# Reciprocal deviations in two halves of three rows, in a kernel with a written-out order for every engine

## The chip, the cores and the metric

The kernel runs on one core of a Trainium2 chip. A core has a matrix engine (TensorE, PE in the profile, with its weight loads as PEld), three engines for element-wise work (VectorE, DVE; ScalarE, ACT; GpSimd, POOL), a sync engine (SP) that here issues every transfer, and 16 DMA engines. The engines run their own instruction streams and meet at semaphores. The metric is the device time of one execution in microseconds (us); lower is better.

## The reference: chunk-selected attention, then a gated MLP

The inputs are q, k and v of 4 batches, 8 heads, 768 positions and 64 elements per head, and the weights of a gated MLP. The reference computes, cut to what matters:

```python
k_min, k_max = k_chunks.min(3), k_chunks.max(3)          # chunks of 32 positions
ub = maximum(q * k_min, q * k_max).sum(-1)                # bound per query and chunk
sel = the 6 chunks with the highest ub, causal            # per query
attn = softmax(where(sel & causal, q @ k.T / 8, -1e9)) @ v
x = attn with its 8 heads side by side                    # 4 x 768 x 512
u, v = halves of gelu_tanh(x @ w_in)                      # 512 columns each
v_n = (v - mean(v)) / sqrt(var(v) + 1e-6) * g_ln          # per row of 512
out = x + (u * (w_sg @ v_n + b_sg)) @ w_out
```

The change concerns `1 / sqrt(var(v) + 1e-6)`: one number for each of the 768 rows of a batch. On the chip these are 6 columns of 128 partitions, a tile of 128x6.

## The kernel before

**Pairs.** The 32 (batch, head) combinations are worked off as 16 pairs of heads, 4 pairs to a batch. For a pair the kernel loads q, k and v, transposes k and q on PE (`kside`, `qside`; both through `rows_T`, line 545), copies the transposed tiles out of PSUM on ACT or DVE (`evac`, lines 451 and 454), takes minimum and maximum per chunk on DVE (line 643, four reductions for a pair), subtracts them on POOL (`wsub`, line 662), takes max(q, 0) on POOL (`rel`, line 676) and casts q to bf16 on POOL (`qcast`, line 683). `select` and `select_full` then do the bound `ub` on PE (line 713 for pairs 0 to 3, line 760 for the later ones, which go two at a time), transpose it (lines 723 and 769), find the sixth-highest value (lines 730 and 780), compare (736, 785) and transpose back into the mask `Dt` (740, 788). The scores follow on PE (lines 874 and 880, or 834), exp on ACT (889 or 840), the zeroing above the diagonal on POOL (896, 845), the product with v on PE (912, 919), and the division by the sum on DVE (927, 929).

**Batches.** After its four pairs, a batch goes through `moe_h` and `moe_g`: the v half of the first matmul on PE (line 961, six row tiles), gelu on ACT (965), the statistics on DVE (970 and 972), variance plus epsilon on DVE (974), the power of -0.5 on POOL (976), and on DVE the normalised rows `vhat` (996), one instruction for each of the six row tiles. The u half is line 1007 on PE and 1012 on ACT. Then comes the spatial matmul on PE (1024), which reads all six `vhat` tiles, its scaling and gating on DVE (1042, 1046), the output matmul on PE (1058), the residual addition on DVE (1067) and the store (1072). The output of the last row tile of the last batch is written in two halves of 256 columns.

**Stores of PSUM.** The scores have two PSUM tiles of their own (PSC); everything else on PE shares four (PSG). Which step takes which is a written-out list (`slots`).

**The order.** Nothing is ordered by the loops alone. Each step is a numbered op, made by `P.op` with its engine, what it reads and what it writes. `TABLE` holds for each of the five queues (pe, act, dve, pool, sp) the list of op numbers in the order in which that engine runs them, and `P.link` puts a semaphore wait wherever an op needs another engine's result. An engine therefore never passes a step that waits. Before the first k transpose PE runs ten spare matmuls on a zeroed tile (`filler`, line 376).

**The start.** POOL makes constant tiles: among them a mask tile `INDF` (line 418), a bf16 identity `identB` (line 387) and some zeroed rows (line 810). In the list of POOL these stand between the steps of pairs 0 and 1: op 91 (cast of q, pair 1), 90 (`rel`, pair 1), 209 (zeroing, line 810), 8 (`identB`), 16 (`INDF`), 85 (`wsub`, pair 1), 108 (`wsub`, pair 2). In PE's list op 184, the third of the six scores steps of pair 0, stands just ahead of op 93, the bound of pair 1.

**Numbers of the ops.** `moe_h` makes two ops for the deviations of a batch in the kernel before (`var` and `rstd`), so that each op behind them in the program has the same number in every queue's list.

Of the kernel before, what the change touches and what calls it, by code (L numbers as in the profile page):

```python
# [6 lines left out]
ALU = mybir.AluOpType  # L7
# [253 lines left out]
def _build(nc, ctx, q, k, v, w_in, g_ln, w_sg, b_sg, w_out, out):  # L261
# [60 lines left out]
    INIT2 = 0  # L322
    K2R = "dma"
# [153 lines left out]
    def wsg_load(j):  # L477
# [4 lines left out]
        if WSGT == "f32":  # L482
            for hf in range(2):
                t = ps_g.tile((0, 1, 2, 3))

                def tr(e, t=t, dst=dst, hf=hf):
                    for x in range(3):
# [7 lines left out]
                     [("wsgT", j, hf)], [t], 1)  # L495
            return
# [455 lines left out]
    def moe_h(b):  # L952
# [3 lines left out]
        for qt in range(NT):  # L956
            t = ps_g.tile((0, 1, 2, 3))

            def hv(e, t=t, qt=qt):
# [14 lines left out]
        P.op("dve", lambda d: d.tensor_scalar(rstd[s][:], mv[s][:, :, 1], 1e-6, None, op0=ALU.add), (75, 150),  # L974
             ("var", b), reads=[("mv", s, qt) for qt in range(NT)], writes=[("rstd", s)])
        P.op("pool", lambda g: g.tensor_tensor(rstd[s][:], rstd[s][:], neghalf[:], op=ALU.pow), (1290, 1340),
             ("rstd", b), reads=[("rstd", s), "neghalf"], writes=[("rstd", s)])
# [6 lines left out]
        for qt in range(NT):  # L984
# [10 lines left out]
            else:  # L995
# [3 lines left out]
                     (456, 548), ("vhat", b, qt), port=True, reads=[("vg", qt), ("mv", s, qt), ("rstd", s)],  # L999
# [16 lines left out]
    def moe_g(b):  # L1016
        s = b % 2
        for tg in range(2):
# [31 lines left out]
            for qt in range(3 * tg, 3 * tg + 3):  # L1050
                cuts = (0, DM // 2, DM) if LAST and (b, qt) == (B - 1, NT - 1) else (0, DM)
                for x, (c0, c1) in enumerate(zip(cuts, cuts[1:])):
# [19 lines left out]
                    P.op("sp", lambda e, qt=qt, ob=ob, c0=c0, c1=c1: e.dma_start(  # L1072
# [48 lines left out]
    for p in range(4, NP + 4):  # L1121
# [38 lines left out]
    "act": (  # L1160
# [10 lines left out]
    "dve": (  # L1171
# [99 lines left out]
```

## Time and profile before

| what | value |
|---|---|
| runs | 213.49 us median of 3 (213.32 to 213.72) |
| the profiled execution's own time | 213.23 us |
| its span, first to last instruction | 211.5 us |
| around the span | 1.7 us |
| granted TensorE clock, mean over the span | 1.000 |
| PE, DVE, ACT, POOL busy | 94%, 87%, 71%, 50% of the span |

The page gives the busy time of each engine and the costliest groups of instructions, by line of the kernel. The view of windows gives busy time for stretches of the span. The view of waits says which line waited for which other engine's line, in total, how often, and the longest. The chain is followed back from the last instruction. The timeline lists start and length of merged runs of instructions, with the idle time ahead of them in square brackets. In rows of groups, "x24" is a count, and a row such as "128x6 f32<-128x6 f32" gives output and input shapes. A busy PE in the profile includes the time in which its matmuls are pipelined.

### The profile page before, as it was taken

Reading aid. Unit: us, or ns where it says so; the run is one execution under the profiler, and the core shown is the slowest. Engines: PE = TensorE matmul, PEld = TensorE weight load, DVE = VectorE, ACT = ScalarE, POOL = GpSimd, SP = SyncE. Lnnn points to the kernel's source line nnn. Section 1 sums busy time; section 2 is a strip of 40 time slices with the busy share of each in tenths; the row PEclk is TensorE's granted clock in tenths of the full one; section 3 lists DMA queues with packets and bytes.
Section 4 is the critical chain, followed back from the end, with each engine's and each line's share of the span. In section 5 each row is a group of like instructions: output and inputs, shape, how many; then the busy total and the mean of one; then the engine's idle time right before and its main releaser. Section 6 shows DMA issues by size and latency. Waiting matters only on the chain.

```text
span 211.5 us, 5892 instructions
## 1 busy us (share of the span) xinstructions
PE 198.9 (94%) x2319; PEld 133.8 (63%) x2319; DVE 184.1 (87%) x523; ACT 150.1 (71%) x227; POOL 105.4 (50%) x157
## 2 busy tenths in 40 slices
PE   7778989889999999999999999999997999999993
PEld 2455757755676668788456777787454777545652
DVE  4597998879999999899999999997599488788994
ACT  2786989947797668799849698999858886263000
POOL 5563967799615849675631754294583143001000
PEclk9999999999999999999999999999999999999999
DMA  7999999999059997949899899648633512410136
GB/s 147 218 218 197 286 198 288 330 276 230 1 150 253 230 239 203 221 104 267 199 180 221 175 227 226 153 122 113 128 86 62 129 37 40 152 47 10 42 149 248
DMA packets 94266, 35.96 MB, mean 170 GB/s; under 512 B 87584, under 2 KB 89376, under 8 KB 94240
## 3 DMA queue, kind: packets, MB, share of 16 engines
q1 hardware_dynamic: 94240, 35.60, 75.8%
q8 instruction: 18, 0.29, 0.6%
q14 instruction: 8, 0.07, 0.1%
HBM read 24.82 MB, written 6.34 MB: 147 GB/s over the span
## 4 chain that ended last, share of the span: by engine, by line
PE 76%; ACT 11%; POOL 5%; DMA 2%; DVE 2%; issue 1%; SPq 1%; DVEq 0%
PE PSG L1024 15%; PE PSC L834 12%; PE PSG L1007 10%; PE PSG L1058 9%; PE PSG L961 8%; PE PSG L545 7%; ACT E L889 5%; PE PSG L912 5%; PE PSG L760 3%; PE PSG L919 2%; ACT KA L451 2%; PE PSC L874 1%; ACT IND L415 1%; PE PSG L713 1%; DMA Wg<-scr_dram 1%
## 5 line engine op out<-in xcount | busy, mean ns | idle before, releaser
L840 ACT ACTIVATE E<-PSC 128x1024 bf16<-128x1024 f32 (+1 forms) x72 | 63.0, 924 | 9.7 <-PE PSC L834 9.4
L834 PE MATMUL PSC<-QA,KA 128*128 128x128 bf16 (+2 forms) x336 | 38.2, 246 | 1.6 <-ACT E L840 1.5
L1024 PE MATMUL PSG<-wsgT,vhat 128*128 128x384 bf16 x192 | 34.3, 326 | 0.0
L643 DVE TENSOR_REDUCE W<-PSG 128x12 f32<-128x384 f32 x56 | 28.0, 543 | 4.3 <-PE PSG L545 4.3
L834 PEld LDWEIGHTS PSC<-QA,KA 128*128 128x128 bf16 x336 | 24.1, 98 | 9.8 <-ACT E L840 4.3
L845 POOL TENSOR_SCALAR_AFFINE_SELECT E<-E 128x768 bf16<-128x768 bf16 x24 | 20.5, 864 | 19.6 <-ACT E L840 19.4
L683 POOL CAST QA<-qT 64x768 bf16<-64x768 f32 (+1 forms) x28 | 24.1, 864 | 9.4 <-PE PSC L834 4.9
L1012 ACT ACTIVATE uT<-PSG 128x384 bf16<-128x384 f32 x32 | 15.1, 489 | 17.5 <-PE PSG L1007 17.4
L1024 PEld LDWEIGHTS PSG<-wsgT,vhat 128*128 128x128 bf16 x192 | 18.4, 98 | 10.7
L1058 PE MATMUL PSG<-woutb,uT 128*128 128x512 bf16 (+1 forms) x100 | 23.8, 371 | 0.0
L889 ACT ACTIVATE E<-PSC 128x1024 bf16<-128x1024 f32 (+1 forms) x24 | 21.0, 916 | 3.6 <-PE PSC L880 3.4
L1007 PE MATMUL PSG<-xT,winb 128*128 128x384 bf16 x128 | 23.4, 326 | 0.0
L961 PE MATMUL PSG<-winb,xT 128*128 128x512 bf16 x96 | 22.5, 380 | 1.0 <-DVE U L775 0.7
L965 ACT ACTIVATE vgb<-PSG 128x512 f32<-128x512 f32 x24 | 14.1, 598 | 12.1 <-PE PSG L961 12.1
L1042 DVE SCALAR_TENSOR_TENSOR PSG<-PSG,glnT,bsgbc 128x384 f32<-128x384 f32 x32 | 19.5, 617 | 2.8 <-PE PSG L1024 2.6
L912 PE MATMUL PSG<-vx,E 128*128 128x65 bf16 x480 | 19.7, 194 | 0.0
L912 PEld LDWEIGHTS PSG<-vx,E 128*128 128x128 bf16 x480 | 17.8, 97 | 1.8 <-DVE XS L929 0.2
L970 DVE BATCH_NORM_STATS2 stats<-vgb 128x6 f32<-128x512 f32 x24 | 15.9, 682 | 3.1 <-ACT vgb L965 2.8
L929 DVE TENSOR_TENSOR XS<-PSG,rden 128x384 bf16<-128x384 f32 x32 | 17.5, 551 | 0.7
L1007 PEld LDWEIGHTS PSG<-xT,winb 128*128 128x128 bf16 x128 | 12.2, 98 | 9.0 <-ACT uT L1012 0.9
L451 ACT ACTIVATE KA<-PSG 128x384 bf16<-128x384 f32 (+1 forms) x34 | 16.5, 492 | 1.7 <-DVE W L643 1.6
L1046 DVE TENSOR_TENSOR uT<-PSG,uT 128x384 bf16<-128x384 f32 x32 | 16.9, 551 | 0.5
(93 smaller groups left out, 342.4 us busy)
## 6 DMA issues: line engine op xcount, KB each, us to landing
kn<-in_k_dram SPq DMA_DIRECT2D x32, 192.0 KB, 4.4
qn<-in_q_dram SPq DMA_DIRECT2D x32, 192.0 KB, 4.5
vn<-in_v_dram SPq DMA_DIRECT2D x16, 384.0 KB, 5.4
out_dram<-osb SPq DMA_DIRECT2D x18, 256.0 KB, 2.6
uT<-in_moe_w_sg_dram SPq DMA_DIRECT2D x4, 384.0 KB, 5.0
vgb<-in_moe_w_in_dram SPq DMA_DIRECT2D x3, 512.0 KB, 7.6
out_dram<-vgb SPq DMA_DIRECT2D x5, 256.0 KB, 2.1
QA<-Dt SPq DMA_DIRECT2D x24, 36.0 KB, 2.2
```

The lines of the kernel that those rows point to most:

```text
L451: P.op("act", lambda e: e.activation(dst(), src(), ACTF.Copy), act(n), tag, reads=reads, writes=writes, ps=ps, shift=shift)
L643: P.op("dve", lambda d, m=m, op=op, src=src, h0=h0, h1=h1: d.tensor_reduce(W[w][:, m, 12 * h0:12 * h1].rearrange("p (h c) -> p h c", h=h1 ...
L683: P.op("pool", lambda g, i=i, r0=r0, r1=r1: g.tensor_copy(QA[w][i or 0][r0:r1, :], qT[r][r0:r1, :]), gps(S, 250 if i == 1 else 150), ("qca ...
L834: r = e.matmul(t.ap()[:, o:o + n], KA[w][i][:, 128 * kb:128 * kb + 128], QA[w][i][:, q0:q0 + n], start=True, stop=True)
L840: P.op("act", lambda e, t=t, c0=c0, c1=c1, i=i: e.activation(E[es][:, i, c0:c1], t.ap()[:, 0:c1 - c0], ACTF.Exp, scale=SCALE), act(c1 - c0 ...
L845: P.op("pool", lambda g, ev=ev: g.affine_select(ev, ev, pattern=[[0, NT], [1, 128]], compare_op=ALU.is_ge, fill=0.0, base=0, channel_multi ...
L889: P.op("act", lambda e, t=t, c0=c0, c1=c1, n=n: e.activation(E[es][:, :, c0:c1], t.ap().rearrange("p (i x) -> p i x", i=2)[:, :, 0:n], ACT ...
L912: r = e.matmul(t.ap()[:, 65 * qb:65 * qb + 65], E[es][:, i, a:a + 128], vx[w][:, kb, i, :], start=first, stop=False, skip_group_check=True)
L961: r = e.matmul(t.ap()[:, 0:F], xT[s][:, dk, 128 * qt:128 * qt + 128], winb[:, dk, F:DFF], start=(dk == 0), stop=(dk == NDK - 1))
L1007: r = e.matmul(t.ap()[:, 0:TG], winb[:, dk, 128 * fb:128 * fb + 128], xT[s][:, dk, TG * tg:TG * tg + TG], start=(dk == 0), stop=(dk == NDK ...
L1024: r = e.matmul(t.ap()[:, 0:TG], vhat[s][:, sb, 128 * fb:128 * fb + 128], wsgT[:, sb, TG * tg:TG * tg + TG], start=(sb == 0), stop=(sb == N ...
L1058: r = e.matmul(t.ap()[:, 0:c1 - c0], gT[s][:, fb, 128 * qt:128 * qt + 128], woutb[:, fb, c0:c1], start=(fb == 0), stop=(fb == NF - 1))
```

## The change

The variance op and the power op of a batch are each replaced by two ops, for row tiles 0 to 2 and 3 to 5, and each `vhat` instruction now depends on its own half only. There are therefore four ops per batch instead of two, 8 more in all (1308 instead of 1300), and the numbers of all ops behind the first batch's deviations shift by 2, behind the second's by 4, and so on. Two further lists that are added (`WSTD`, `STQ`) are empty, so the code that they guard makes no op. The lists of all five queues, the PSUM slots and the filler (11 spare matmuls instead of 10) are new.

```diff
+    LNG = ((0, 3), (3, 6))
+    WSTD = ()
+    STQ = ()
...
-        P.op("dve", lambda d: d.tensor_scalar(rstd[s][:], mv[s][:, :, 1], 1e-6, None, op0=ALU.add), (75, 150),
-             ("var", b), reads=[("mv", s, qt) for qt in range(NT)], writes=[("rstd", s)])
-        P.op("pool", lambda g: g.tensor_tensor(rstd[s][:], rstd[s][:], neghalf[:], op=ALU.pow), (1290, 1340),
-             ("rstd", b), reads=[("rstd", s), "neghalf"], writes=[("rstd", s)])
+        for a0, a1 in LNG:
+            rn = [("rstd", s, qt) for qt in range(a0, a1)]
+            P.op("dve", lambda d, a0=a0, a1=a1: d.tensor_scalar(rstd[s][:, a0:a1], mv[s][:, a0:a1, 1], 1e-6, None, op0=ALU.add),
+                 (75, 150), ("var", b, a0), reads=[("mv", s, qt) for qt in range(a0, a1)], writes=rn)
+            P.op("pool", lambda g, a0=a0, a1=a1: g.tensor_tensor(rstd[s][:, a0:a1], rstd[s][:, a0:a1], neghalf[:, a0:a1], op=ALU.pow),
+                 (200 + 190 * (a1 - a0), 250 + 190 * (a1 - a0)), ("rstd", b, a0), reads=rn + ["neghalf"], writes=rn)
...
-                     (456, 548), ("vhat", b, qt), port=True, reads=[("vg", qt), ("mv", s, qt), ("rstd", s)],
+                     (456, 548), ("vhat", b, qt), port=True, reads=[("vg", qt), ("mv", s, qt), ("rstd", s, qt)],
...
     "pool": (
-        "5 11 4 6 2 20 3 326 21 12 19 56 51 57 7 91 90 209 8 16 85 108 197 113 58 196 114 164 159 128 249 165 "
...
+        "2 11 3 12 20 4 19 21 6 56 51 5 57 90 85 7 16 197 108 91 113 114 58 165 164 196 261 159 207 92 248 "
...
-        "47:10 77:2"),
+        "47:11 77:2"),
```

In the lists, the steps that the prediction speaks of stand as follows. (The names are those of the ops' tags: `kmm` a reduction of line 643, `hv` and `hu` the matmuls of lines 961 and 1007, `wst` the transpose of a tile of w_sg.)

| queue | before | after |
|---|---|---|
| POOL, pair 1 | cast of q, `rel`, zeroing, `identB`, `INDF`, `wsub` | `rel`, `wsub`, zeroing, `INDF`, a diagonal of pair 0, `wsub` of pair 2, cast of q |
| DVE, pairs 0 and 1 | compare of pair 0, its back transpose, two `kmm` of pair 1 (with one of pair 2 between) | compare of pair 0, `kmm` of pair 1, back transpose of pair 0, `kmm` of pair 1 |
| PE, pair 1 | scores step 184 of pair 0, then the bound of pair 1 | the bound of pair 1, then that scores step |
| SP, start | k, k, q, q of pair 0 | k, q, k, q of pair 0 |
| PE, batch 0 | `hu`, then the sixth `hv` | two `hu` and a `wst`, then the sixth `hv`, then that `hu` |
| POOL, batch 0 | w_sg cast 4, power, w_sg cast 5 | w_sg cast 4, a cast of q, power of the first half, w_sg cast 5, power of the second half |
| POOL, select of pairs 14, 15 | copies `wmin`, `wsub`, then `rel` of pair 15, `wmin`, `wsub` | `rel` of pair 15 and four other steps first, then the four copies together |
| SP, select of pairs 14, 15 | four loads of `Wg` follow the third x transpose | a load of v stands ahead of them |
| DVE, batch 3 | six statistics, variance, an addition (line 1067), six `vhat`, two additions | variance of the first half after four statistics, two `vhat` among the rest, variance of the second half, an addition, the last three `vhat`, two additions |
| PE and DVE, end | row tile 4, then the second half of row tile 5 | the second half of row tile 5, then row tile 4 |

More of the change, by code (lines that the diff above doesn't have):

```diff
@@ L495, in wsg_load @@
                      [("wsgT", j, hf)], [t], 1)
+            return
+        if j in WSTD:
+            wb = vhat[0][:].rearrange("p a b -> p (a b)")[:, S * (j % 4):S * (j % 4) + S]
+            wn = [("vhat", 0, y) for y in range(S * (j % 4) // F, (S * (j % 4) + S - 1) // F + 1)] + [("wv", j % 4)]
+            cast(wb, dst, S, ("wsc", j), [("stg", j % 4)] + names, wn)
+            P.op("sp", lambda e: e.dma_start(wsgT[:, :, 128 * j:128 * j + 128], wb, transpose=True), dmac(TRI), ("wtr", j),
+                 reads=wn, writes=[("wsgT", j, hf) for hf in range(2)], dma=f"trw{j}", xfer=TRX)
             return
@@ L1071, in moe_g @@
                         reads=[t] + [("XS", b % 2, hh) for hh in range(c0 // 64, c1 // 64)] + ([("vg", qt)] if x else []), writes=on, ps=[t])
-                    P.op("sp", lambda e, qt=qt, ob=ob, c0=c0, c1=c1: e.dma_start(
+                    P.op("act" if b in STQ else "sp", lambda e, qt=qt, ob=ob, c0=c0, c1=c1: e.dma_start(
                         bass.AP(out.tensor, (b * S + 128 * qt) * DM + c0, [[DM, 128], [1, c1 - c0]]), ob[:, c0:c1]), dmac(),
@@ L1143 @@
     "pe": (
[16 rows of a table removed]
-    "act": (
[10 rows of a table removed]
-    "dve": (
[17 rows of a table removed]
-    "pool": (
[14 rows of a table removed]
[16 rows of a table added]
+    "act": (
[10 rows of a table added]
+    "dve": (
[17 rows of a table added]
+    "pool": (
[15 rows of a table added]
     "slots": (
-        "1032323020021303233221230011010031120221010100231021031011000330001010010233121033010211230223301210"
-        "3203312003101011201131111010101232023111010033313011001101302220120223131002232210323032110230110100"
-        "3020000001113132310210011131131010010301021021113331320232031210300311101100021100111111000031100110"
-        "23203231130003222312023012101231"),
+        "3210103201021020001323021211010123310021110000321022031011002330203010010133130021011210023233121310"
+        "2201332112001011200120001110010332132111010033312311001101302322020222032113011330013032130012010100"
+        "3120010111013032320210011013121010011322021023131313002103233210312032101100231100110211100010101100"
+        "12220210110220312100320312131203"),
     "filler": (
-        "47:10 77:2"),
+        "47:11 77:2"),
 }
```

111 rows, old and new, of the table TABLE are left out of this document.

## The prediction

> **What bounds the kernel now.** I began with busy time by stretch of the span, from the view of windows. The columns are the length, then the busy time of PE, PEld, DVE, ACT and POOL, the granted clock, the DMA share and the GB/s.
>
> ```profile
> 5.00:47.00 42.00, 36.11 (x634) 26.06 (x632) 35.69 (x112) 34.37 (x52) 29.39 (x45) 1.00 1.14 254
> 47.00:145.00 98.00, 97.97 (x1147) 69.79 (x1146) 94.21 (x279) 79.66 (x124) 55.89 (x77) 1.00 0.90 187
> 145.00:165.00 20.00, 17.84 (x172) 10.28 (x171) 14.99 (x51) 16.10 (x25) 11.73 (x19) 1.00 0.43 93
> 165.00:208.30 43.30, 43.28 (x363) 26.29 (x360) 36.47 (x74) 18.73 (x27) 6.07 (x7) 1.00 0.28 85
> ```
>
> PE is the bound from 47 to 145 and from 165 to 208.3: 97.97 of 98.00 and 43.28 of 43.30. There an edit can only lose. Its idle time lies in the first 47 us (42.00 - 36.11 = 5.9 between 5 and 47) and between 145 and 165 (2.2). Next came the view of waits for PE, first from 5 to 50, then from 145 to the end (total, times, longest).
>
> ```profile
> PE PSG L713 <- POOL W L662: 1.8, 2, 1.2
> PE PSC L874 <- ACT E L889: 1.3, 2, 0.7
> ```
>
> ```profile
> PE PSC L834 <- ACT E L840: 1.5, 1, 1.5
> PE PSG L760 <- POOL W L618: 0.3, 1, 0.3
> ```
>
> None of these names the deviations. What waits for them is in the view of the tile `rstd` (min/median/max in ns, then the first and last start):
>
> ```profile
> L974 DVE TENSOR_SCALAR rstd<-mv x4: 170/174/406, 56.0 to 189.6; 128x6 f32<-128x6 f32 x4
> L976 POOL TENSOR_TENSOR rstd<-rstd,neghalf x4: 1327/1346/1769, 56.5 to 189.9; 128x6 f32<-128x6 f32 x4
> ...
>   DVE vhat L996: 0.6, 2
> ```
>
> DVE loses 0.6 us to the power in the whole run, in two batches; PE, the bound, loses nothing that the profile shows. So the halves as such can bring at most part of 0.6 us of DVE, and the time hangs on the new lists.
>
> **The halves.** They add four DVE instructions (4 x 0.174 = 0.70 us) and four on POOL. What a half power costs no row shows. At the least it is half, 0.67; at the most it is whole, 1.35. A POOL operation on four times as many elements stands in the view of line 662:
>
> ```profile
> L662 POOL TENSOR_TENSOR W<-W x6: 227/236/242, 9.0 to 40.0; 128x24 f32<-128x24 f32 x6
> ```
>
> So what an instruction costs whatever its size is at most 0.24 there, and I take 0.24 + (1.35 - 0.24) / 2 = 0.79. The Trainium skill, GPSIMD Engine Reference, section Instruction dispatch, speaks against the change: each instruction is broadcast to eight cores, goes through a software dispatcher on each, and ends when all eight are done, a cost that two halves pay twice. The row of 0.24 bounds that cost here; if the power were all dispatch, its half would cost 1.35, the upper end, and that case is a rival below.
>
> **The start: the queue of POOL ahead of pair 1's bound.** The largest wait of the start, 1.2 us, is PE's bound of pair 1 (line 713) waiting for line 662. The chain shows why, as start, length and step:
>
> ```profile
> 12.68 0.82 POOL QA L683
> 13.50 0.64 POOL rT L676
> 14.14 0.35 POOL QA L810
> 14.49 0.25 POOL identB L387
> 14.73 1.60 POOL INDF L418
> ...
> 16.58 1.29 PE PSG L713 x18
> ...
> 20.71 0.40 PE PSC L874 x8
> ```
>
> The new list moves the cast (0.82), the zeroing (0.35), `identB` (0.25) and `INDF` (1.60), together 3.0 us, behind `wsub` of pair 1; only `rel` stays ahead. What is late next is the last reduction of pair 1 on DVE, from the timeline:
>
> ```profile
> 11.15 0.83 DVE L730 MAX8 m<-U 128x8 f32<-128x16 f32 x9
> 12.01 0.46 DVE L736 TENSOR_TENSOR Dn<-U,m 128x288 bf16<-128x288 f32 x1
> 12.50 0.48 DVE L740 STREAM_TRANSPOSE Dt<-Dn 128x288 bf16<-128x288 bf16 x1
> 12.90 1.45 DVE L643 TENSOR_REDUCE W<-PSG 128x12 f32<-128x384 f32 x3
> ```
>
> Behind the compare (end 12.47) come a reduction (1.45 / 3 = 0.48), the back transpose (0.48) and the other reduction (0.5): 13.97, and with 0.24 for `wsub` the bound could start at 14.2 instead of 16.58, 2.4 earlier. That is one end. What counts, though, is the exp on ACT, which the scores feed:
>
> ```profile
> 13.71 2.85 ACT L889 ACTIVATE E<-PSC 128x1024 bf16<-128x1024 f32 x3 [0.71 <-PE PSC L880]
> 18.13 2.38 ACT L889 ACTIVATE E<-PSC 128x256 bf16<-128x256 f32 x3 [1.18 <-PE PSC L880]
> ```
>
> The idle 1.18 in the second row is the same wait, and it goes. Against it, the back transpose of pair 0 comes 0.48 later, so the first exp may, and the bound (1.29) stands before a scores step that ran at 14.85, which then starts at 14.2 + 1.29 = 15.5, 0.65 later. All of it counted, the gain is 1.18 - 0.48 - 0.65 = 0.05. I take 1.0, near the row of the wait, because the two delays fall into stretches in which later exps still queue, and because every later select begins earlier too. Ends: -2.4 and, from the first rival below, +1.1.
>
> **Other edits at the start.** The eleventh spare matmul and the second half of k, now the third load instead of the second:
>
> ```profile
> 1.26 4.23 PE L376 MATMUL PSC<-warm 128*128 128x512 bf16 x11 [1.26 <-DVE warm L373]
> ...
> 6.37 0.88 PE L545 MATMUL PSG<-identF,qn 128*128 128x128 f32 x6 [0.22 <-DMA qn<-in_q_dram]
> ```
>
> One more costs 4.23 / 11 = 0.38. But the q transposes wait 0.22 for the fourth load, which is the fourth in both lists, so 0.22 is covered and 0.16 could show if the cover is gone; I take 0, with ends 0 and +0.2.
>
> **47 to 145.** All five queues are permuted, and PE has nothing to win. In batch 0 the sixth `hv` goes behind more `hu`, and the second half power behind a w_sg cast; rows from the timeline and from the view of `vhat`:
>
> ```profile
> 58.20 0.94 POOL L447 CAST wsb<-uT 128x768 bf16<-128x768 f32 x1 [0.33 <-PE PSG L503]
> ...
> 58.85 2.40 DVE L996 TENSOR_SCALAR vhat<-vgb,mv,rstd 128x512 bf16<-128x512 f32 x5
> ```
>
> ```profile
> L1024 PE MATMUL PSG<-wsgT,vhat x23: 326/326/327, 61.8 to 65.9; 128*128 128x384 bf16 x23
> ```
>
> The last `vhat` ends at 61.25 and PE starts on it at 61.8. With 0.79 the second power ends at 58.20 + 0.94 + 0.79 = 59.9, and four `vhat` of 0.48 end at 61.85: just in time. I take 0; ends 0 and +0.6 (the whole power).
>
> **145 to 165.** The wait of 0.3 on line 618 is the select of pairs 14 and 15: its copies stood around a `rel`, now they stand together, while a load's issue goes ahead of the four small ones. I take -0.2; ends -0.3 (the wait) and +0.3 (if that issue shows instead). The 1.5 on exp stays: in the new list, too, a third scores step follows two, with two PSUM tiles, behind the last gelu.
>
> **Batch 3.** Here no other batch covers the chain:
>
> ```profile
> 187.53 0.60 ACT L965 ACTIVATE vgb<-PSG 128x512 f32<-128x512 f32 x1 [0.27 <-PE PSG L961]
> ...
> 191.25 2.82 DVE L996 TENSOR_SCALAR vhat<-vgb,mv,rstd 128x512 bf16<-128x512 f32 x6 [0.21 <-POOL rstd L976]
> ...
> 194.47 1.79 PE L1024 MATMUL PSG<-wsgT,vhat 128*128 128x384 bf16 x10
> ```
>
> ```profile
> L970 DVE BATCH_NORM_STATS2 stats<-vgb 128x6 f32<-128x512 f32 x6 | 4.0, 680 | 0.6 <-ACT vgb L965 0.5
> L972 DVE BATCH_NORM_AGGREGATE mv<-stats 128x2 f32<-128x6 f32 x6 | 1.0, 178 | 0.1
> ```
>
> The slack of PE is 194.47 - (191.25 + 2.82) = 0.40. From the last gelu (188.13) the new DVE list holds some 0.2 of a running statistic, two statistics (1.36), four aggregates (0.71), two variances (0.34), an addition (0.69, below) and six `vhat` (2.82), 6.1 in all, so it ends at 194.25; the second power (0.79) covers itself with the addition but for 0.1 and two semaphores. I take +0.2; ends 0 and +0.8 (the whole power).
>
> **The end.** PE's last step becomes a 512-column tile:
>
> ```profile
> 203.79 4.49 PE L1058 MATMUL PSG<-woutb,uT 128*128 128x512 bf16 x24
> ...
> 207.88 1.02 DVE L1067 TENSOR_TENSOR vgb<-PSG,XS 128x512 f32<-128x512 f32 x2 [0.28 <-PE PSG L1058]
> ```
>
> ```profile
> L1067 DVE TENSOR_TENSOR vgb<-PSG,XS 128x512 f32<-128x512 f32 x5 | 3.4, 687 | 0.4 <-PE PSG L1058 0.3
> L1067 DVE TENSOR_TENSOR vgb<-PSG,XS 128x256 f32<-128x256 f32 x2 | 0.8, 414 | 0.0
> ```
>
> The last addition ended at 208.90. Now it starts at PE's end, 208.28, and takes 0.69: 209.0. I take +0.1; ends 0 and +0.27, the difference of the two sizes.
>
> **The sum.** -1.0 + 0 + 0 - 0.2 + 0.2 + 0.1 = -0.9. The profiled execution's own time is 213.23 (span 211.5 and 1.7 around it), which gives 212.3; it lies 0.26 below the median of the runs, 213.49, so as a median I forecast 212.6.
>
> **The rivals.** First, slower: POOL's queue turns against pair 1. Its cast of q now stands behind `wsub` of pair 2, which waits for a reduction that DVE does after pair 1's search. From the start of pair 1's bound that is 1.29 on PE, then on DVE a transpose (0.48), two copies and a reduction (0.5 each) and the search (0.83), then 0.24 and 0.82 on POOL: 5.2 us. The scores of pair 1 began at 20.71, so this decides as soon as the bound starts later than 15.5, for instance because a PSUM slot or a reduction holds it. If it starts no earlier than before, at 16.58, the early term is +1.1 instead of -1.0: 213.49 + 1.1 - 0.2 + 0.2 + 0.1 = 214.7; at the point itself 213.6. For it speaks that POOL now has three waits in a row there, against it the 14.2 above.
>
> Second, no early gain: the loads set the pace.
>
> ```profile
> DMA packets 94266, 35.96 MB, mean 170 GB/s; under 512 B 87584, under 2 KB 89376, under 8 KB 94240
> ```
>
> From 5 to 47 the DMA share is 1.14, full. Then a faster start only waits for the weights and the early term is 0: 213.6. Against it, the largest waits of PE there name POOL and ACT. The Trainium skill, DMA: Bandwidth & Descriptors, section Specifications, would favour this rival: pieces under 512 B do not reach line rate, and 87584 of the 94266 packets are under that.
>
> Third, the power does not halve: 1.35 each. Then batch 0 pays 0.6 and batch 3 another 0.5: 213.7. That is what the rule on dispatch would give; the row of 0.24 speaks against it.
>
> Fourth, the whole 2.4 of the bound's start comes through: 211.2.
>
> **How the numbers follow.** My forecast has a chance of 0.40, its own range 211.9 to 213.0; the fourth rival 0.10. The first has 0.33, the second 0.12, the third 0.05. A measurement tells about 0.2% from no change, 0.43 us. Faster is then 0.40 + 0.10 = 0.50; the second and third, and the near edge of the first, make 0.17 for the same, the rest, 0.33, is slower. The range reaches from 211.8, which leaves most of the fourth out, to 214.6, just short of the first at its full price.
>
> **What would show it.** Right: line 713's longest wait for POOL falls below 0.5 and the second exp gap (1.18) is gone; the first `hv` starts about 1 us sooner; the half power takes about 0.8; PE stays full from 47 to 145; the last addition is 512 wide. Wrong: a new PE wait for ACT or POOL before 25 us (first rival), hv at an unchanged time (second), a half power above 1.1 with a wait at line 1024 (third), or any PE wait between 47 and 145, where I priced none.

## The result, and the profile after

The changed kernel takes 211.12 us (median of 4 executions, 210.75 to 212.06) against 213.44 for the kernel before beside it: a ratio of 0.9896, 95% interval 0.9863 to 0.993, some 2.3 us less. The forecast was 212.6 with a range of 211.8 to 214.6, so the time lies below the range. A second set of 11 executions, run with the experiments, gave 211.99 (210.87 to 212.96), just inside the range, and a ratio of 0.9927 (0.9906 to 0.9949): the gain is 1.6 to 2.3 us, where 0.9 was forecast. Executions of one kernel come in a faster and a slower state, and all times and ratios are of the faster. The profiled execution took 211.06, with a span of 209.3.

Line numbers of the changed kernel are 3 to 12 higher: L662 is L672, L713 is L723, L805 is L815, L889 is L899, L976 is L988, L1067 is L1079. Kernels edited from the one before keep the old numbers. First the busy time by stretch, columns as before:

```profile
5.00:47.00 42.00, 38.83 (x646) 27.30 (x646) 36.73 (x133) 34.59 (x54) 31.59 (x52) 1.00 1.17 258
47.00:145.00 98.00, 97.08 (x1141) 69.11 (x1146) 92.46 (x266) 80.69 (x125) 55.43 (x79) 1.00 0.84 184
145.00:165.00 20.00, 18.35 (x180) 11.00 (x180) 14.72 (x53) 16.15 (x24) 9.98 (x17) 1.00 0.60 115
165.00:206.00 41.00, 40.78 (x339) 24.48 (x341) 35.01 (x73) 17.61 (x26) 5.94 (x7) 1.00 0.25 83
```

PE is busy 38.83 instead of 36.11 in the first 47 us: 2.7 us of idle time have gone there, more than the whole gain; from 145 to 165 PE is busy 0.5 more (the same windows hold work that stood some 2 us later before). The waits of PE, from 5 to 50 (total, times, longest):

```profile
PE PSG L971 <- DVE U L785: 0.9, 1, 0.9
PE PSC L884 <- ACT E L899: 0.6, 2, 0.4
PE PSG L555 <- ACT qT L454: 0.5, 1, 0.5
PE PSG L555 <- issue: 0.4, 1, 0.4
PE PSG L956 <- DVE xT L457: 0.3, 1, 0.3
PE PSC L884 <- DVE Dt L750: 0.2, 1, 0.2
```

and from 145 to the end:

```profile
PE PSC L844 <- ACT E L850: 1.5, 1, 1.5
```

The wait of the bound for POOL (1.8, longest 1.2) has gone, that for exp fell from 1.3 to 0.6, and the wait of 0.3 in the select of pairs 14 and 15 has gone; the 1.5 on exp has stayed. The start in the timeline (POOL, PE and ACT):

```profile
12.11 0.67 POOL L686 TENSOR_SCALAR rT<-qT 128x576 f32<-128x576 f32 x1 [2.39 <-ACT qT L454]
13.46 0.24 POOL L672 TENSOR_TENSOR W<-W 128x24 f32<-128x24 f32 x1 [0.69 <-DVE W L653]
13.74 1.64 POOL L421 TENSOR_TENSOR INDF<-IND 128x768 bf16<-128x768 bf16 x1
...
13.95 0.69 PE L723 MATMUL PSG<-qT,W 64*32 64x288 f32 x8
...
17.22 2.22 ACT L899 ACTIVATE E<-PSC 128x256 bf16<-128x256 f32 x3
...
19.49 0.40 PE L884 MATMUL PSC<-QA,KA 64*128 64x128 bf16 x8
```

`INDF` stands behind `wsub`, the bound of pair 1 starts at 13.95 instead of 16.58, the second exp gap (1.18) is gone, and the scores of pair 1 start at 19.49 instead of 20.71. The first bound and the first `hv`, of before and then of the changed kernel:

```profile
9.30 0.69 PE L713 MATMUL PSG<-qT,W 64*32 64x288 f32 x8 [0.57 <-POOL W L662]
...
46.88 1.04 PE L961 MATMUL PSG<-winb,xT 128*128 128x512 bf16 x4 [0.65 <-DVE U L775]
```

```profile
8.93 0.69 PE L723 MATMUL PSG<-qT,W 64*32 64x288 f32 x8
...
44.83 0.81 PE L971 MATMUL PSG<-winb,xT 128*128 128x512 bf16 x3 [0.88 <-DVE U L785]
```

The last row lacks its first record (x3 instead of x4, and 0.23 more idle time), so that `hv` starts at 44.60, 2.3 earlier: the whole gain is there before the first batch. The deviations, in the view of the tile `rstd`:

```profile
L986 DVE TENSOR_SCALAR rstd<-mv x8: 136/166/326, 52.9 to 189.4; 128x3 f32<-128x3 f32 x8
L988 POOL TENSOR_TENSOR rstd<-rstd,neghalf x8: 848/860/1081, 53.3 to 189.7; 128x3 f32<-128x3 f32 x8
...
  DVE vhat L1008: 0.7, 2
```

A half power takes 0.86, and DVE waits as long for the power as before (0.7 against 0.6). Batch 3 and the end:

```profile
190.55 1.46 DVE L1008 TENSOR_SCALAR vhat<-vgb,mv,rstd 128x512 bf16<-128x512 f32 x3 [0.37 <-POOL rstd L988]
...
192.18 1.14 PE L1036 MATMUL PSG<-wsgT,vhat 128*128 128x384 bf16 x6
...
206.03 0.69 DVE L1079 TENSOR_TENSOR vgb<-PSG,XS 128x512 f32<-128x512 f32 x1 [0.28 <-PE PSG L1070]
```

The last `vhat` ends at 192.01, 0.17 before PE starts on it; the last addition is 512 wide.

### The profile page after: what moved, and what is told of

It reads as the page before. It is cut to its first block, busy times and chain, and to the rows that moved or that the text cites. A ratio compares the mean times of both kernels' runs of the same rounds, so it can differ in the third digit from the quotient of the medians.

```text
span 209.3 us, 5887 instructions
## 1 busy us (share of the span) xinstructions
PE 198.8 (95%) x2306; PEld 133.2 (64%) x2320; DVE 181.6 (87%) x527; ACT 150.5 (72%) x227; POOL 105.3 (50%) x161
## 2 busy tenths in 40 slices
DMA packets 94266, 35.96 MB, mean 172 GB/s; under 512 B 87584, under 2 KB 89376, under 8 KB 94240
## 3 DMA queue, kind: packets, MB, share of 16 engines
HBM read 24.82 MB, written 6.34 MB: 149 GB/s over the span
## 4 chain that ended last, share of the span: by engine, by line
PE 82%; DVE 7%; ACT 6%; DMA 1%; issue 1%; POOL 0%; DVEq 0%
PE PSG L1036 15%; PE PSC L844 12%; PE PSG L1019 10%; PE PSG L971 10%; PE PSG L1070 9%; PE PSG L555 7%; PE PSG L922 5%; PE PSG L770 3%; ACT E L899 3%; PE PSC L379 2%; PE PSG L929 2%; PE PSC L884 2%; PE PSG L723 2%; DMA QA<-Dt 1%; DVE W L653 1%
## 5 line engine op out<-in xcount | busy, mean ns | idle before, releaser
L844 PE MATMUL PSC<-QA,KA 128*128 128x128 bf16 (+2 forms) x336 | 37.6, 246 | 2.1 <-ACT E L850 1.5
L693 POOL CAST QA<-qT 64x768 bf16<-64x768 f32 (+1 forms) x28 | 22.9, 821 | 4.8 <-ACT qT L454 2.3
L1054 DVE SCALAR_TENSOR_TENSOR PSG<-PSG,glnT,bsgbc 128x384 f32<-128x384 f32 x32 | 19.4, 618 | 4.3 <-PE PSG L1036 4.1
L899 ACT ACTIVATE E<-PSC 128x1024 bf16<-128x1024 f32 (+1 forms) x24 | 20.8, 920 | 2.8 <-PE PSC L890 2.6
L971 PE MATMUL PSG<-winb,xT 128*128 128x512 bf16 x92 | 21.5, 379 | 1.0 <-DVE U L785 0.9
L1070 PE MATMUL PSG<-woutb,uT 128*128 128x512 bf16 (+1 forms) x90 | 21.8, 369 | 0.6
L698 POOL CAST vx<-vn 128x768 bf16<-128x768 f32 x16 | 13.3, 835 | 13.9 <-DMA vn<-in_v_dram 13.7
L980 DVE BATCH_NORM_STATS2 stats<-vgb 128x6 f32<-128x512 f32 x24 | 15.9, 681 | 3.7 <-ACT vgb L975 3.5
L988 POOL TENSOR_TENSOR rstd<-rstd,neghalf 128x3 f32<-128x3 f32 x8 | 7.1, 889 | 23.7 <-DVE rstd L986 23.6
```

What stands on the lines that cost most here:

```text
L693: P.op("pool", lambda g, i=i, r0=r0, r1=r1: g.tensor_copy(QA[w][i or 0][r0:r1, :], qT[r][r0:r1, :]), gps(S, 250 if i == 1 else 150), ("qca ...
L844: r = e.matmul(t.ap()[:, o:o + n], KA[w][i][:, 128 * kb:128 * kb + 128], QA[w][i][:, q0:q0 + n], start=True, stop=True)
L899: P.op("act", lambda e, t=t, c0=c0, c1=c1, n=n: e.activation(E[es][:, :, c0:c1], t.ap().rearrange("p (i x) -> p i x", i=2)[:, :, 0:n], ACT ...
L971: r = e.matmul(t.ap()[:, 0:F], xT[s][:, dk, 128 * qt:128 * qt + 128], winb[:, dk, F:DFF], start=(dk == 0), stop=(dk == NDK - 1))
L1054: P.op("dve", lambda d, t=t, fb=fb, tg=tg: d.scalar_tensor_tensor(t.ap()[:, 0:TG], t.ap()[:, 0:TG], glnT[:, fb:fb + 1], bsgbc[:, TG * tg:T ...
L1070: r = e.matmul(t.ap()[:, 0:c1 - c0], gT[s][:, fb, 128 * qt:128 * qt + 128], woutb[:, fb, c0:c1], start=(fb == 0), stop=(fb == NF - 1))
```

## The experiments

The times are medians; the ratio, of means, is to the kernel before, run on the same chip. The last column is the time from the start of the first bound to the start of the last exp of pair 3 in the profiled execution. It leaves out when the first loads landed, which shifts the first bound by up to 0.8 us between profiles. It belongs to one execution, which can lie anywhere among those of its kernel: `wsub` first was profiled at 212.72, the longest of its seven, the changed kernel in its second set at 210.97, the second shortest of eleven. Five profiles of the same new start give 30.76 to 31.34, so a difference of 0.6 says nothing.

| kernel | us | ratio, 95% interval | bound 0 to last exp of pair 3 |
|---|---|---|---|
| before | 213.4 to 213.6 | 1 | 33.05 |
| changed | 211.12 | 0.9896 (0.9863 to 0.993) | 30.76 |
| changed, again | 211.99 | 0.9927 (0.9906 to 0.9949) | 30.77 |
| halves in the old order | 213.70 | 1.0011 (1.0003 to 1.002) | 33.08 |
| new order, whole deviations | 214.37 | 1.0044 (1.003 to 1.0058) | 31.34 |
| new order, halves in batch 2 alone | 212.69 | 0.9971 (0.9956 to 0.9986) | 31.30 |
| new start, rest old | 211.70 | 0.9928 (0.9916 to 0.994) | 30.80 |
| old start, rest new | 213.67 | 1.001 (1.0001 to 1.0019) | 32.98 |
| `wsub` of pair 1 first | 211.98 | 0.9942 (0.9921 to 0.9963) | 31.97 |
| changed, POOL's start old | 213.90 | 1.0052 (1.0024 to 1.0081) | 34.68 |
| new only up to 19.4 us | 214.42 | 1.0049 (1.0021 to 1.0077) | 33.08 |
| copies behind mask 2 | 213.76 | 1.0017 (1.0006 to 1.0029) | 33.32 |
| `wsub` first, copies behind mask 2 | 212.61 | 0.9968 (0.9953 to 0.9983) | 32.43 |
| copies behind mask 3 | 213.67 | 1.0011 (0.9995 to 1.0026) | 33.25 |
| `wsub` first, copies behind mask 3 | 212.87 | 0.997 (0.995 to 0.9991) | 32.89 |
| changed, copies ahead | 212.38 | 0.9946 (0.9929 to 0.9964) | 32.54 |
| `rel` of pair 15 first | 212.80 | 0.9976 (0.9966 to 0.9987) | 33.05 |
| three edits | 212.36 | 0.9957 (0.9932 to 0.9982) | 32.13 |
| four edits | 211.78 | 0.9924 (0.9895 to 0.9953) | 30.57 |
| changed, copies later | 211.30 | 0.9895 (0.988 to 0.9909) | 30.56 |

**The halves or the lists, the start or the rest.** The halves in the old order (the old lists, with the new pairs of ops side by side in the places of the old ones):

```diff
-  "dve":  ... var(b) ...      "pool": ... rstd(b) ...
+  "dve":  ... var(b,0) var(b,3) ...      "pool": ... rstd(b,0) rstd(b,3) ...
```

> Theory (the gain is made by the new lists in the first 47 us, the halves as such bring nothing): 213.4 to 213.8, the time of the kernel before or up to 0.4 more, since the two half powers together take 0.86 + 0.86 = 1.72 instead of 1.35 and the last one stands ahead of batch 3's last vhat. Rival (the halves themselves bring the gain, because DVE starts on vhat earlier): 211 to 212, and the wait of vhat for the power falls clearly below 0.6.

Measured 213.70, 0.2 more than before: the halves by themselves bring nothing. The converse, the new lists with one power at the place of the second half:

```diff
-    LNG = ((0, 3), (3, 6))
+    LNG = ((0, 6),)
...
-  "dve": ... var(b,0) ... vhat(b,0) ... var(b,3) ... vhat ...
+  "dve": ... var(b) ... vhat(b,0) vhat ...
```

> The new lists with one variance and one power for all six rows. Theory (the lists bring the gain): 211.0 to 211.5, the time of the changed kernel or up to 0.4 more where vhat waits for the whole power in batch 3. Rival (the halves bring it): 212.5 to 213.5.

Measured 214.37: the theory missed, the kernel is slower than before. From 158 to 168 PE waits for

```profile
PE PSG L1036 <- DVE vhat L1008: 1.7, 1, 1.7
```

This is batch 2. The new list of DVE puts the compare of pairs 14 and 15 ahead of the last aggregate, and that of POOL puts two copies and a cast between the half powers; a whole power comes only behind all of it. Another 0.4 is lost in the same way in batch 0. So the new lists are paid for by the halves, though the halves do not pay alone. With the halves in batch 2 and whole powers in the other three:

```diff
-        for a0, a1 in LNG:
+        for a0, a1 in (LNG if b == 2 else ((0, NT),)):
```

> The changed kernel with the halves in batch 2 alone; batches 0, 1 and 3 have one variance and one power, at the place of the second half. Theory (in the new lists the halves matter where the mask of pairs 14 and 15 goes ahead of the last aggregate, which is batch 2; batch 0 loses 0.4 at its first spatial matmul): 211.5 to 212.4. Rival (they matter in all batches): 213.0 to 214.5.

212.69 lies between the two: the wait of 1.7 is gone, one of 0.4 at the spatial matmul is left in batch 0, and the rest is not told apart. Next the two ways of joining old and new lists at the first `hv`:

```diff
-  all queues: old list, old PSUM slots
+  all queues: steps that the changed kernel starts before 44.8 us in the new order and slots, then the old list
```

> The kernel before, with the new lists only for the steps that the changed kernel starts before 44.8 us (its first hv); everything behind has the old order and whole deviations. Theory (the gain is made before the first hv and then carried): 211.0 to 211.6, and the first hv starts at about 44.8 instead of 46.9. Rival (the later lists bring it): 212.8 to 213.5.

> The changed kernel, with the old lists for the steps that the kernel before starts before 46.8 us; the halves and all later lists are the new ones. Theory: 213.1 to 213.6, the later lists being worth 0 to 0.3. Rival (the later lists bring the gain): 211.0 to 211.8.

211.70 with the new start alone, 213.67 with everything new but the start: each 0.1 above its theory's range and far from its rival. So 1.5 us (0.0072 of 213.4; interval 1.3 to 1.8) are made before the first `hv`. Whether the rest adds to that is not shown: the two sets of the changed kernel lie 0.6 below 211.70 and 0.3 above it, and on the old start the rest gains nothing.

**The queue of POOL ahead of pair 1's bound.** The changed kernel once more, as a base, then the edit that the prediction priced, alone in the kernel before, and its reverse in the changed kernel:

> The changed kernel once more, unedited, with more executions, as the base for the runs beside it: 210.8 to 211.4, a ratio to the kernel before of 0.989 to 0.990 with a narrower interval than the first.

```diff
   "pool": (before)
-    ... 7 91 90 209 8 16 85 108 ...
+    ... 7 90 85 91 209 8 16 108 ...
```

> The kernel before with one edit in the list of POOL: rel and wsub of pair 1 go ahead of the cast of q, the zeroing, identB and INDF. Theory A (the start is worth 1.6 to 1.7 and this queue makes it): 211.7 to 212.2, the bound of pair 1 starting at about 15. Theory B (the start needs the other lists too, which put the reductions, the scores and the exps in the order that uses the earlier bound): 212.7 to 213.4, with the wait of the bound on POOL gone and the exps of pair 1 at most 0.8 earlier.

```diff
   "pool": (changed)
-    ... 57 90 85 7 16 197 108 91 113 ...
+    ... 57 7 91 90 209 8 16 85 197 108 113 ...
```

> The changed kernel with those steps of POOL put back ahead of wsub of pair 1 (zeroing, cast of q, rel, identB, INDF). Theory A: it loses the whole early gain, 212.7 to 213.2. Theory B: it loses only the part that hangs on this queue, 0.3 to 1.0: 211.4 to 212.1.

The base missed its range: 211.99. The edit alone gives 1.2 us (interval 0.8 to 1.7), by the time theory A. Its median, 211.98, is that of the changed kernel on the same chip, and the intervals overlap: by time, this one move is not told apart from the whole change. In the last column it gains 33.05 - 31.97 = 1.1, less than the 2.3 of the changed kernel, but in an execution 0.7 above its median.

The reverse costs more than either theory said, and its executions form two groups. Six have a mean granted clock of 1.0 and take 213.36 to 214.08, the whole gain and up to 0.9 above theory A's range; the other six have 0.992 and take 215.33 to 216.78. The profiled one (215.68) is of the second group, so that its 34.68 holds lost clock too (see the last section). There the bound of pair 1 stands ahead of the third scores step of pair 0, waits for POOL, and the exps of pair 0 wait behind it (PE, then ACT):

```profile
16.67 0.96 PE L723 MATMUL PSG<-qT,W 64*32 64x288 f32 x8 [1.96 <-POOL W L672]
...
19.66 1.02 ACT L899 ACTIVATE E<-PSC 128x1024 bf16<-128x1024 f32 x1 [3.42 <-PE PSC L890]
```

Then the new lists only for the steps up to pair 1's mask:

```diff
-  all queues: old list
+  all queues: steps that the changed kernel starts before 19.4 us in the new order and slots, then the old list
```

> The kernel before with the new lists only for the steps that the changed kernel starts before 19.4 us (bound, search and mask of pair 1). Theory A (the gain is made at pair 1 and carried): 211.6 to 212.1. Theory B (pair 1 gives about 0.8, the rest comes from the orders of pairs 2 and 3): 212.4 to 213.0, with exps of pair 1 about 0.8 earlier and the first hv not more than 0.8 earlier.

214.42 decides nothing. Five of the eight executions have a mean granted clock of 0.992 (214.27 to 215.28), the other three take 212.93 to 213.66. And the joined PSUM slots made a wait that neither kernel has, for a copy that had not yet left its tile; from the profiled execution (212.94):

```profile
22.41 0.69 PE L713 MATMUL PSG<-qT,W 64*32 64x288 f32 x8 [1.97 <-ACT KA L451]
```

**The masks of pairs 2 and 3.** In the kernel before, two copies of `INDF` into KA stand ahead of the mask of pair 2 on DVE, which nothing reads before pair 4 (DVE and POOL, in order of time):

```profile
24.91 0.82 POOL L447 CAST wsb<-uT 128x768 bf16<-128x768 f32 x1
24.96 0.99 DVE L805 COPY KA<-INDF 64x768 bf16<-64x768 bf16 x1
...
26.24 1.01 DVE L805 COPY KA<-INDF 64x768 bf16<-64x768 bf16 x1
...
27.37 0.43 DVE L740 STREAM_TRANSPOSE Dt<-Dn 128x288 bf16<-128x288 bf16 x1
```

The new list has one copy ahead of that mask (0.58) and the two far behind. They were moved in two steps, first behind the mask of pair 2, then behind that of pair 3, each without and with the edit of POOL:

```diff
   "dve": (behind mask 2)
-    ... 118 208 119 260 28 200 204 120 205 216 ...
+    ... 118 119 28 200 204 120 205 208 260 216 ...
   "dve": (behind mask 3)
-    ... 118 208 119 260 28 ... 258 257 269 ...
+    ... 118 119 28 ... 258 257 208 260 269 ...
```

> The kernel before with one edit in the list of DVE: the two copies of INDF into KA (line 805; 0.99 and 1.01 us each in the profile of before, where a copy of the same size takes 0.36 elsewhere) that stand ahead of the mask of pair 2 go behind it. Nothing needs them before pair 4. Theory C (these copies are the part of the start that the queue of POOL leaves over): the mask of pair 2 comes up to 2.0 earlier and the time falls by 0.4 to 0.9, to 212.6 to 213.1. Rival (the exps in front of pair 2 hide it): 213.3 to 213.6.

> Both edits at once in the kernel before: rel and wsub of pair 1 first on POOL, and the two copies of INDF behind the mask of pair 2 on DVE. Theory C (the two together are the early gain): 211.4 to 211.9, as with all new lists up to the first hv (211.7). Rival (the gain needs the orders of ACT and PE too): 212.0 or more, no better than the edit of POOL alone.

> The kernel before with the two copies of INDF (line 805) that stand ahead of the mask of pair 2 put behind the mask of pair 3 and its next steps on DVE. Theory C (DVE's work ahead of the masks of pairs 2 and 3 is the rest of the early gain): the mask of pair 3 comes 1.0 to 1.6 earlier and the time is 212.3 to 212.9. Rival (exp on ACT sets the pace there): 213.2 to 213.6.

> That edit together with rel and wsub of pair 1 first on POOL. Theory C (the two make up the early gain): 211.5 to 212.0, as with all new lists up to the first hv. Rival (the orders of ACT and PE carry the rest): 212.1 to 212.7.

All four miss theory C. Without the edit of POOL, the mask of pair 2 does come 1.0 earlier. With it, the mask comes 15.9 behind the first bound whether the copies are moved or not, because they take a third of their time there even where they stood (`wsub` first):

```profile
24.27 0.33 DVE L805 COPY KA<-INDF 64x768 bf16<-64x768 bf16 x1
...
24.89 0.35 DVE L805 COPY KA<-INDF 64x768 bf16<-64x768 bf16 x1
...
25.62 0.44 DVE L740 STREAM_TRANSPOSE Dt<-Dn 128x288 bf16<-128x288 bf16 x1
```

In the first new place the copies then hold the mask of pair 3, and in the second a reduction of pair 5. Behind that one stands a copy of k on ACT, ahead of the last four exps of pair 3; from the kernel with three edits (these two and `rel` of pair 15, below):

```profile
37.85 0.49 ACT L451 ACTIVATE KA<-PSG 64x384 bf16<-64x384 f32 x1 [0.93 <-DVE W L643]
```

The reverse in the changed kernel:

```diff
   "dve": (changed)
-    ... 25 205 206 119 26 ... 
+    ... 25 205 206 208 119 260 26 ...
```

> The changed kernel with those two copies put back ahead of the mask of pair 2. Theory C: it loses 0.5 to 1.0 against the changed kernel (211.1 to 212.0 in its two sets of runs), the mask of pair 3 coming 0.7 to 1.5 later: 212.2 to 212.8. Rival: no loss, 211.1 to 212.0.

212.38 is within theory C's times, but its interval overlaps that of the changed kernel's second set. The mask of pair 2 is late again, as before the change:

```profile
24.30 1.62 DVE L815 COPY KA<-INDF 64x768 bf16<-64x768 bf16 x2
25.84 0.44 DVE L746 TENSOR_TENSOR Dn<-U,m 128x288 bf16<-128x288 f32 x1
26.21 1.01 DVE L815 COPY KA<-INDF 64x768 bf16<-64x768 bf16 x1
27.17 0.45 DVE L750 STREAM_TRANSPOSE Dt<-Dn 128x288 bf16<-128x288 bf16 x1
```

**The select of pairs 14 and 15.**

```diff
   "pool": (before)
-    ... 959 998 1001 1006 1000 ...
+    ... 959 1006 998 1001 1000 ...
```

> The kernel before with rel of pair 15 ahead of the four copies on POOL. Theory (the select of pairs 14 and 15 is held by that step): the gap of PE ahead of the bound of pair 14 falls from 0.79 to about 0.44, and the time by 0.3 to 0.5: 212.9 to 213.2. Rival (a load or the reductions are late next): 213.3 to 213.6.

212.80, 0.5 less (0.3 to 0.7) and 0.1 below the theory's range. In the kernel before the bound of pair 14 starts after a wait, here without one; before, then this kernel:

```profile
152.51 0.72 PE L760 MATMUL PSG<-qT,W 64*32 64x288 f32 x16 [0.31 <-POOL W L618]
```

```profile
152.13 0.71 PE L760 MATMUL PSG<-qT,W 64*32 64x288 f32 x16
```

**The edits together.** First POOL's edit, the copies behind mask 3, and `rel` of pair 15 first; then also the copies further back, and that copy of k on ACT behind the exps of pair 3:

> The kernel before with three edits of the lists and whole deviations: those two, and rel of pair 15 ahead of the four copies on POOL. Theory (these three places hold the gain, the halves none): 211.0 to 211.6. Rival (the gains do not add up, or the halves are needed): 212.0 or more.

```diff
   "act": (before; 271 is the last copy of k of pair 5)
-    ... 360 271 362 358 356 270 364 274 ...
+    ... 360 362 358 356 270 364 271 274 ...
```

> The three edits, with the two copies of INDF further back (behind the division of pair 2), and a fourth: on ACT the last copy of k of pair 5 goes behind the exps of pair 3. Whole deviations, all other steps as in the kernel before. Theory (these four places hold the gain of the change): the last exp of pair 3 about 2 earlier than before, 211.0 to 211.7. Rival (the orders of the other steps or the halves are needed): 212.0 to 212.5, no better than three edits.

Three edits give 212.36, as the rival said; four give 211.78, between theory and rival, with 30.57 in the last column, no more than the changed kernel's 30.76. In the executions with the clock at 0.996 or more (10 of 12, and 5 of 6), the medians are 211.99 and 211.50. So four moves of a few steps in the old lists, with whole deviations, give a time that the intervals do not separate from the changed kernel's; but nor do they separate the one move on POOL. Which of the two moves that four edits have over three brings the 1.6 in the column was not tried. Last, the changed kernel without its own copies ahead of the masks:

```diff
   "dve": (changed)
-    ... 25 205 206 119 26 120 200 ... 170 258 171 ...
+    ... 25 205 119 26 120 206 200 ... 170 171 258 ...
```

> The changed kernel with its two copies of INDF that still stand ahead of the masks of pairs 2 and 3 (0.58 and 0.36) put right behind them. Theory C (DVE's work ahead of a mask is on the path): 0.2 to 0.6 less than the changed kernel, 210.7 to 211.6. Rival (exp sets the pace by then, or the copies collide with POOL in the new place): 211.1 to 212.2, the spread of the changed kernel itself.

211.30: the mask of pair 2 comes 0.7 earlier and the first `hv` 0.2, and the time is not told apart from the changed kernel's. It is the fastest that is known with a narrow interval; nothing beats the changed kernel for certain.

## Why the prediction was wrong, step by step

- **The bound (right but for one wait).** PE's idle time in the first 47 us was named as the place of the gain, the halves as worthless by themselves: 213.70 with the halves alone. That 47 to 145 costs nothing held but for one new wait of 0.3 on a transfer (`QA<-Dt`), where the prediction had priced none; PE's busy time there is 0.9 lower with 6 records fewer, some of which are missing ones. What was missed is that the new lists need the halves in batch 2.
- **The start (the step that failed).** "I take 1.0" stood for the whole new start; the new start alone gave 1.5 (1.3 to 1.8). For the edit that it was worked out from it was near: 1.2 (0.8 to 1.7) in the times. The step priced one queue at one pair as if that were the start. From the first bound to the last exp of pair 3 the new lists gain 33.05 - 30.77 = 2.3 in the profiles, 1.2 of it up to the scores of pair 1. The sum had no term for what comes behind, at the masks of pairs 2 and 3: DVE's work ahead of them, the copy of k on ACT ahead of exps. That these make the difference is argued from the column, not shown by the times, in which the move on POOL alone is not told apart from the whole change; what carries the rest stays open. Some of the 2.3 is given back by the first `hv`: from the first bound to it, 46.88 - 9.30 = 37.58 before and 44.60 - 8.93 = 35.67 after (with the missing record), a gain of 1.9. The two copies of 0.99 and 1.01 could not be seen in the view of waits, which names for PE only who came last.
- **Spare matmul and load order (taken as 0).** The first bound starts at 8.93 instead of 9.30. So it did in five of the nine profiles with the new start (8.86 to 8.94; the other four 9.34 to 9.61), and in none of those with the old one (9.30 to 9.70). This probably adds up to 0.4; the load order was not tried by itself.
- **145 to 165 (mis-sized).** -0.2 was taken, 0.5 measured: one step, `rel` of pair 15, gives it alone. The prediction read the wait of 0.31; but with everything ahead of it unchanged the bound starts 0.38 earlier, since a wait is counted from the modelled end of pipelined matmuls. On the old start this order is there too and shows no gain (213.67); why stays open.
- **Batch 3 (mis-sized).** +0.2 was taken, 0 measured: the last `vhat` ends 0.17 before PE needs it. Three of the six `vhat`, not two, stand ahead of the second half's variance, and from the end of the last gelu PE starts on `vhat` after 6.34 us in both kernels.
- **The end (right).** From PE's end to the end of the last addition it is 206.72 - 205.98 = 0.74 against 208.90 - 208.28 = 0.62: +0.1.
- **The sum.** With the measured sizes it is -1.5 - 0.5 + 0 + 0.1 = -1.9 instead of -0.9, which lies between the two sets (-1.6 and -2.3). That the terms add up is not shown.
- **The half power.** 0.79 was taken, 0.86 measured; the bounds, 0.67 and 1.35, hold it. From 1.35 for six columns and 0.86 for three, a column costs 0.16 and an instruction 0.37 besides. The Trainium skill, GPSIMD Engine Reference, section Instruction dispatch, names a cost that two halves pay twice: the runs agree in kind (1.72 against 1.35), but not to the length of the third rival.
- **The rivals.** The fourth, "the whole 2.4 comes through", came nearest in time (211.2) for a reason that did not hold: at pair 1's scores 1.2 had come through, and the rest came at pairs 2 and 3. The first did not come about. Where POOL's start was put back in the changed kernel, the bound of pair 1 does start as late as before (16.67); the executions at the full clock then take 213.36 to 214.08, less than the rival's 214.7, and the longer ones lose clock, which the rival did not price. The second fell: DMA moves the same 87584 packets under 512 B, its share from 5 to 47 is 1.17, and PE does 2.7 us more work in that time; pieces under 512 B, on which the Trainium skill, DMA: Bandwidth & Descriptors, section Specifications, bears, did not set the pace.

## What to carry to other kernels

When a whole order is exchanged, list for each deadline (each mask, each exp) what stands ahead of it on its queue before and after, over the whole stretch in which the bounding engine is idle, and not only at the longest wait. A step that is not needed yet costs time ahead of a deadline, but moved behind it it may hold the next one: the two copies gained nothing in either new place. Before explaining what a single edit leaves over, compare it with the whole change on the same chip; here the intervals left nothing over. Ask where the profiled execution lies among its kernel's, and compare executions of the same granted clock. A split that gains nothing alone can still carry an order that needs it.

## What the runs showed of the hardware

**A difference of 0.07 us decides 0.67.** Two kernels with the same order up to there, `wsub` first with the copies behind mask 3 and the three edits, in DVE's and POOL's timeline:

```profile
27.20 0.84 POOL L688 CAST vx<-vn 128x768 bf16<-128x768 f32 x1 [0.39 <-DMA vn<-in_v_dram]
27.23 1.03 DVE L805 COPY KA<-INDF 64x768 bf16<-64x768 bf16 x1
```

```profile
27.23 0.36 DVE L805 COPY KA<-INDF 64x768 bf16<-64x768 bf16 x1
27.27 1.01 POOL L688 CAST vx<-vn 128x768 bf16<-128x768 f32 x1 [0.42 <-DMA vn<-in_v_dram]
```

In the first, POOL's cast, which waits for a load of v, starts 0.07 sooner and so ahead of DVE's copy, and the copy takes 1.03 instead of 0.36; in the other order POOL waits, 1.01 instead of 0.84. The Trainium skill, SBUF — State Buffer, section SBUF: two separate sides, says that the two share a pair of ports, and that whichever starts first, GpSimd or a VectorE instruction that uses the pair, has it for its whole instruction; the rows agree. With one more such meeting the mask of pair 3 came 0.96 later (31.97 against 31.01). So the gain of such an order depends on where loads land, and one profile is no measure of 0.5 us here.

**The granted clock fell behind waits of 1 to 2 us, in some executions.** In the profiled execution of the four edits, the longest of its six (213.46; the others 211.12 to 212.46), PE waits for a load of q, and the windows behind it (columns as above) show the clock:

```profile
40.48 0.52 PE L545 MATMUL PSG<-identF,qn 128*128 128x128 f32 x3 [1.02 <-DMA qn<-in_q_dram]
...
41.66 0.71 PE L545 MATMUL PSG<-identF,qn 128*128 128x128 f32 x3 [0.67 <-DVE wsgT L454]
```

```profile
36.00:40.00 4.00, 3.44 (x77) 2.59 (x73) 3.92 (x8) 4.00 (x6) 3.31 (x6) 1.00 1.05 330
40.00:44.00 4.00, 2.86 (x34) 2.59 (x35) 3.16 (x6) 2.81 (x5) 2.88 (x4) 0.74 1.13 326
44.00:48.00 4.00, 3.11 (x64) 2.16 (x63) 2.89 (x8) 0.20 (x1) 3.75 (x6) 0.83 1.03 262
```

The clock lost is 0.26 x 4 + 0.17 x 4 = 1.7 us, what 3.4 us at half speed lose. The Trainium skill, TensorE: Matmul & The Clock Gate, section Part 1: The HAM clock gate, gives windows of about 3.4 us in which the clock is whole or half, and half after an idle window. The size agrees; but PE waited only 1.0 and 0.7 here, not a whole window. In the changed kernel with POOL's start old, the same follows the wait of 1.96:

```profile
12.00:16.00 4.00, 2.13 (x28) 1.33 (x26) 3.89 (x12) 2.18 (x3) 3.24 (x5) 1.00 1.36 218
16.00:20.00 4.00, 3.33 (x36) 1.89 (x37) 0.93 (x2) 0.58 (x2) 0.61 (x2) 0.62 1.35 220
20.00:24.00 4.00, 3.92 (x52) 2.94 (x52) 3.51 (x18) 3.28 (x5) 2.10 (x4) 0.95 1.08 205
```

That is 0.38 x 4 + 0.05 x 4 = 1.7 us again, and 1.7 is 0.008 of 213, what the executions with a mean of 0.992 lack. They are six of 12 there and five of eight with the new lists up to 19.4 us, and none of the kernel before or the changed kernel. The wait does not always bring the fall: the profiled execution of the new lists up to 19.4 us keeps 1.00 behind its 1.97. That the waits are the cause is argued from these traces, not shown.

In the four edits, the last exp of pair 3 came 2.5 earlier than before the edits, the first `hv` 0.7 later (47.56 with its missing record). Why the load was late in that execution stays open.
